# Row scales read back by three plain transfers; low halves of the attention weights made in one operation, with V loaded to both halves of the partitions

## The chip, the cores and the metric

The kernel runs on one core of a Trainium2 chip. The metric is the device time of one execution in microseconds, as the median of several runs. Five engines work side by side, each through its own list of instructions in order: PE (matrix multiplies, with PEld for its weight loads), DVE, ACT, POOL, and SP, which here issues every DMA.

## The reference

Attention with a threshold, followed by a feed-forward layer:

```python
# q, k, v: (8, 8, 576, 64), all f32
scores = scale * np.matmul(q, k.transpose(0, 1, 3, 2))
thresh = np.max(scores, axis=-1, keepdims=True) - tau
scores = np.where(scores >= thresh, scores, -1000000000.0)
scores = scores - np.max(scores, axis=-1, keepdims=True)
attn = np.exp(scores)
attn = attn / (np.sum(attn, axis=-1, keepdims=True) + 1e-09)
attn_out = np.matmul(attn, v)
...
x = attn_out.transpose(0, 2, 1, 3).reshape(8 * 576, 512)
h = x @ w_in                                   # w_in: (512, 2048)
g = np.maximum(h, 0.0) + np.log1p(np.exp(-np.abs(h)))
out = g @ w_out                                # w_out: (2048, 512)
```

## The kernel before

**Units and tiles.** A unit is one batch entry with two heads; there are 32 of them. A unit has 9 tiles of 128 query rows by 576 keys: tiles 0 to 3 belong to head 0, tiles 5 to 8 to head 1, and tile 4, called M, holds the last 64 rows of both heads. The main loop runs over 288 tiles. `PAT = "RemhlTfpSxfvwp"` gives the steps of one tile `t`, in the order in which they are written:

- `S`: the scores of tile t+3 on PE, into one of two PSUM buffers (`s`).
- `R`, `e`: the row maximum of tile t+2 (`negm`, DVE), its exponentials (`e_all`, ACT) and the threshold (`thr`, ACT).
- `m`: the mask of tile t+1 with its row sums (DVE, reads `s` and `e_all`); after it the PSUM buffer is free for new scores.
- `h`: `weights_hi` of tile t+1: POOL rounds the weights to f16.
- `l`: `weights_lo` of tile t: DVE makes the f16 remainder. Both go into one buffer `e16` of 1152 columns per row, shown in the profile as `e`.
- `T`: `weights_T` of tile t-1: a transposing DMA of that buffer into `eT`.
- `x`: `extras`: the work of the whole unit, spread over its tiles. `f`: a share of the feed-forward matmuls (`h`, `o`). `p`: one point; work that was put off by so many points is done there (two points in a tile).

The first six units (`s.whole`) go another way, with f32 weights transposed on PE, and do not use `weights_hi`, `weights_lo` and `weights_T`. In the other 26 units each block of 128 columns of `e16`, once transposed, is one matmul operand against 128 rows of `vt`: 64 keys as high halves and 64 other keys as low halves in the same block. So `weights_lo` writes the low halves of keys 0 to 511 to columns 640 to 1151 and those of keys 512 to 575 to columns 576 to 639, with two operations.

**V.** `load_v` loads V of the next unit into `vn` (one buffer for these units) in tile 0 of the running unit: one DMA to 128 partitions and two small ones for the last 64 keys. `top_v` takes its largest magnitude on DVE in tile 3, `split_v` scales it on ACT and splits it into f16 halves on POOL (`vt`) in tile 7. `load_v` of the unit after cannot be issued before POOL has read `vn`.

**Row scales.** After the last mask of a unit, `row_scales` makes the reciprocals; in the next unit they are transposed on PE (tile 1), copied by ACT to `rt`, written to HBM (`r_d`) and read back by `load_R` as `R`, each value to 64 partitions. `scale_x` on POOL multiplies the values by them 7 points later. `sums` puts the sum of tile t into column `ORDER[t]`, so that tile M stands last.

**Queries.** `queries` scales the next unit's queries of head 0 on ACT into the single buffer `q0` (shown as `q`), and `swap` exchanges its partition halves by two DMAs, `q<-q`. The scores of the next unit's first tile need them; `S` writes those three tiles ahead. The same for head 1 is `qT<-qT`.

**The order.** SP issues all DMAs in the order of the program, each one waiting for what it needs, so whatever stands behind a waiting DMA waits too. `Queue` and the priorities fix the order on DVE and ACT in the later part. Buffers of `e16`: `HB` in their own pool; from tile 84 on (`TE`) the even tiles of a unit use the three buffers `wi` of the weights instead.

Of the kernel before, what the change touches and what calls it, by code (L numbers as in the profile page):

```python
# [24 lines left out]
P = 128  # L25
# [38 lines left out]
def tile_kernel(ctx: ExitStack, tc: tile.TileContext, q, k, v, tau, w_in, w_out, out):  # L64
# [271 lines left out]

    def load_v(s):

        s.vn = apool.tile([P, 10, D], F32, tag="vt" if s.whole else "vn", bufs=2 if s.whole else 1, name=f"vn_{s.i}")
        load_rows(s, s.vn, v)  # L340
        for i in range(2):
            nc.sync.dma_start(
                s.vn.rearrange("p (h s) d -> p h s d", h=2)[i * SR:(i + 1) * SR, :, NC, :],
                v[s.b, 2 * s.hp:2 * s.hp + 2, SM:S, :].rearrange("h p d -> p h d"),
            )
# [188 lines left out]
    def weights_hi(s, t):  # L534

        pool, tag, bufs = (apool, "e16", HB) if now["tile"] < TE or t % 2 else (wpool, "wi", WB)
        s.e16[t] = h = pool.tile([P, 2 * S], F16, tag=tag, bufs=bufs, name=f"e16_{s.i}_{t}")
        nc.gpsimd.tensor_scalar(out=h[:, 0:S], in0=s.e[t], scalar1=2.0 ** 15, scalar2=1.0, op0=ALU.mult, op1=ALU.mult)  # L538

    def weights_lo(s, t):  # L540
        h, e = s.e16[t], s.e.pop(t)
        for i, o in ((slice(0, SM), slice(S + SR, 2 * S)), (slice(SM, S), slice(S, S + SR))):
            vec.scalar_tensor_tensor(out=h[:, o], in0=e[:, i], scalar=2.0 ** 15, in1=h[:, i],
                                     op0=ALU.mult, op1=ALU.subtract)

    def weights_T(s, t):
        if t in (0, M):
            j = int(t == M)
            s.eT[j] = apool.tile([P, 9, S], F16, tag="eT", bufs=2, name=f"eT_{s.i}_{j}")
        h = s.e16.pop(t)  # L550
        if t == M:
            for j in range(2):
                nc.sync.dma_start_transpose(s.eT[j][:, :, SM:S], h[j * SR:(j + 1) * SR])
            return
        j, c = divmod(t, NC + 1)
        nc.sync.dma_start_transpose(s.eT[j][:, :, c * P:(c + 1) * P], h)

    def values(s, g):
        if g == 0:
            s.xp = apool.tile([P, S], F32, tag="xp", bufs=NX, name=f"xp_{s.i}")  # L560
        j, x0 = g // 2, g % 2 * HS
        o = ps_g.tile([P, 512], F32, tag="g", name=f"pv_{s.i}_{g}")
        order = (0, 5, 1, 6, 2, 7, 3, 8, 4)
        for n, c in enumerate(order):
            nc.tensor.matmul(o[:, 0:HS], s.vt[:, 5 * j + (c if c <= NC else c - NC - 1), :],  # L565
                             s.eT[j][:, c, x0:x0 + HS], start=(n == 0), stop=(n == 8))
# [30 lines left out]
    def load_R(s):  # L597
        s.R = apool.tile([P, S], F32, tag="R", bufs=1, name=f"R_{s.i}")
        rows = s.r_d.rearrange("a p -> (a p)")
        for a, n in ((0, SM), (2 * SM, SR)):  # L600
            nc.sync.dma_start(s.R[:, a and SM:(a and SM) + n],
                              rows[a:a + 2 * n].rearrange("(j n) -> j n", j=2)[:, None, :].to_broadcast([2, D, n]))
# [330 lines left out]
    for s in units:  # L933
# [123 lines left out]
```

## Time and profile before

| | |
|---|---|
| median of 3 runs | 1413.39 us (1407.13 to 1413.59) |
| profiled execution, its own time | 1408.86 us |
| its span | 1407.1 us |
| PE busy | 1281.8 us, 91% |
| DVE busy | 1031.4 us, 73% |
| POOL busy | 920.9 us, 65% |
| ACT busy | 894.3 us, 64% |
| mean granted TensorE clock | 0.968 |

Tiles of the split units (from the seventh on) run from about 233 to 1257 us; ahead of that are the whole units and the preparation of the feed-forward weights, behind it feed-forward work alone. In a view by windows each engine has its busy time in the stretch, then come the granted TensorE clock, the mean busy share of the 16 DMA engines and what they moved. A row of a timeline has start, length, engine, line and operation, and in brackets how long the engine idled before it and what ended that. Instructions made through `Queue` all have its line, L154, and are told apart by their tiles.

### The profile page before, as it was taken

To read this page: it belongs to the slowest core of one execution; us is meant where nothing else is said; L and a number is where in the kernel's file an instruction comes from. 1 tells how busy PE (TensorE), PEld (TensorE's weight loads), DVE (VectorE), ACT (ScalarE), POOL (GpSimd) and SP (SyncE) were. 2 spreads that over 40 slices of the span, in tenths; PEclk is the share of its full clock that TensorE was granted. 3 is DMA by queue.
4 is the path that set the end of the run, shared out by engine and by line. 5 is a ranking of instruction groups with operands and counts; after the bars stand their busy time and mean duration, and the time that the engine had idled before them with its cause. 6 is when DMAs were issued, how large, how long until landed. Compare 5 with 4: busy or idle time off the path is not lost.

```text
span 1407.1 us, 21600 instructions
## 1 busy us (share of the span) xinstructions
PE 1281.8 (91%) x7094; PEld 759.2 (54%) x7094; DVE 1031.4 (73%) x1955; ACT 894.3 (64%) x1695; POOL 920.9 (65%) x1007
## 2 busy tenths in 40 slices
PE   6888898778989898999999999899999999999998
PEld 4555554344555555555555555555665765554455
DVE  6777766598987797789888898789787788761011
ACT  6666687556676667666776666566876667663222
POOL 2566878587776676667766676668767678546242
PEclk9988799999999999999999999999999999999999
DMA  4535333665876778777876786778766755651010
GB/s 140 143 107 126 116 82 95 118 101 109 164 123 115 119 138 140 122 126 127 148 131 116 120 159 125 119 122 160 117 118 114 142 100 124 97 77 40 0 38 16
DMA packets 354369, 158.15 MB, mean 112 GB/s; under 512 B 309297, under 2 KB 335313, under 8 KB 354257
## 3 DMA queue, kind: packets, MB, share of 16 engines
q1 hardware_dynamic: 354256, 156.77, 58.8%
q8 instruction: 56, 0.92, 0.3%
q14 instruction: 57, 0.46, 0.1%
HBM read 56.62 MB, written 10.63 MB: 48 GB/s over the span
## 4 chain that ended last, share of the span: by engine, by line
PE 34%; DVE 24%; ACT 15%; POOL 9%; issue 9%; DMA 6%; SPq 1%; DVEq 0%; POOLq 0%; ACTq 0%
PE o L751 12%; PE h L687 10%; DVE e L154 8%; PE s L455 6%; DVE e_all L154 6%; ACT L154 4%; DVE negm L154 4%; ACT st L154 4%; DMA q<-q 4%; PE pv L565 3%; ACT e_all L154 2%; DVE acc L154 2%; PE pv L524 2%; POOL g L178 2%; DVE xp L154 1%
## 5 line engine op out<-in xcount | busy, mean ns | idle before, releaser
L751 PE MATMUL o<-w_o,g 128*128 128x512 f16 x1728 | 419.3, 389 | 4.8 <-POOL g L178 2.3
L538 POOL TENSOR_SCALAR e<-e_all 128x576 f16<-128x576 f32 x234 | 226.2, 967 | 223.2 <-DVE e_all L154 220.9
L687 PE MATMUL h<-xh,w_i 128*128 128x512 f16 (+1 forms) x1280 | 363.0, 361 | 5.2 <-ACT xp L154 3.5
L154 DVE SCALAR_TENSOR_TENSOR e<-e_all,e 128x512 f16<-128x512 f32 x468 | 343.1, 772 | 14.3 <-POOL e L538 14.2
L154 ACT ACTIVATE e_all<-s,negm 128x576 f32<-128x576 f32 x288 | 213.4, 741 | 208.0 <-DVE negm L154 205.8
L687 PEld LDWEIGHTS <-w_i 128*128 128x128 f16 x1920 | 180.1, 98 | 166.6 <-issue 11.4
L154 DVE TENSOR_REDUCE negm<-s 128x1 f32<-128x576 f32 x288 | 214.6, 746 | 73.5 <-PE s L455 72.6
L154 DVE SCALAR_TENSOR_TENSOR e_all<-s,thr,e_all 128x576 f32<-128x576 f32 x288 | 232.6, 808 | 45.4 <-ACT thr L154 45.2
L751 PEld LDWEIGHTS <-g 128*128 128x128 f16 x1728 | 162.2, 100 | 186.1 <-issue 17.1
L687 PE MATMUL h<-xl,w_i 128*128 128x512 f16 (+1 forms) x640 | 230.9, 361 | 0.5 <-POOL xl L178 0.5
L455 PE MATMUL s<-kT,q 128*128 128x288 f32 x768 | 160.7, 336 | 68.5 <-DVE e_all L154 32.9
L154 DVE SCALAR_TENSOR_TENSOR acc<-o,c,acc 128x512 f32<-128x512 f32 x108 | 80.1, 743 | 164.2 <-PE o L751 146.3
L455 PEld LDWEIGHTS s<-kT,q 128*128 128x128 f32 x768 | 117.5, 198 | 116.5 <-DVE e_all L154 69.9
L178 POOL TENSOR_TENSOR g<-st,g 128x512 f16<-128x512 f32 x144 | 173.7, 1209 | 6.2
L154 ACT ACT_TABLE_LOAD x119 | 152.7, 1283 | 7.8 <-PE h L687 4.1
L177 POOL TENSOR_SCALAR g<-st 128x512 f16<-128x512 f32 x144 | 90.9, 634 | 96.6 <-ACT st L154 96.3
L565 PE MATMUL pv<-eT,vt 128*128 128x288 f16 x936 | 136.7, 291 | 3.8 <-DVE xp L154 3.5
L154 ACT ACTIVATE st<-h,c 128x512 f32<-128x512 f32 x144 | 91.1, 683 | 70.1 <-PE h L687 69.4
L455 PE MATMUL s<-kT,qT 128*128 128x288 f32 x512 | 107.5, 333 | 10.8 <-DVE e_all L154 10.0
L154 ACT COPY xp<-pv 64x288 f32<-64x288 f32 (+3 forms) x134 | 50.6, 382 | 95.0 <-PE pv L565 87.1
L565 PEld LDWEIGHTS <-vt 128*128 128x128 f16 x936 | 86.6, 99 | 38.1 <-issue 7.1
L154 ACT ACTIVATE st<-st,c 128x512 f32<-128x512 f32 x144 | 96.1, 715 | 2.1
(105 smaller groups left out, 1556.9 us busy)
## 6 DMA issues: line engine op xcount, KB each, us to landing
q<-q SPq DMA_DIRECT2D x62, 192.0 KB
kn<-in_k_dram SPq DMA_DIRECT2D x32, 256.0 KB
qn<-in_q_dram SPq DMA_DIRECT2D x32, 256.0 KB
vn<-in_v_dram SPq DMA_DIRECT2D x32, 256.0 KB
wc_i<-in_moe_w_in_dram SPq DMA_DIRECT2D x16, 512.0 KB
R<-r_d SPq DMA_DIRECT2D x32, 256.0 KB
wc_o<-in_moe_w_out_dram SPq DMA_DIRECT2D x16, 512.0 KB
qT<-qT SPq DMA_DIRECT2D x62, 128.0 KB
```

The costliest lines, as they stand in the source:

```text
L154: i = getattr(self.eng, name)(*args, **kwargs)
L177: nc.gpsimd.tensor_scalar(out=hi, in0=x, scalar1=1.0, scalar2=1.0, op0=ALU.mult, op1=ALU.mult)
L178: nc.gpsimd.tensor_tensor(out=lo, in0=x, in1=hi, op=ALU.subtract)
L455: nc.tensor.matmul(sp[:, hf, 0:HS], lhs, s.kT[j][:, hf * HS:(hf + 1) * HS], start=(m == 0), stop=(m == len(parts) - 1))
L524: nc.tensor.matmul(o[0:D, 0:n], s.vn[k_, 5 * j + c, :], h[k_, c, 0:n], start=(c == 0), stop=(c == NC))
L538: nc.gpsimd.tensor_scalar(out=h[:, 0:S], in0=s.e[t], scalar1=2.0 ** 15, scalar2=1.0, op0=ALU.mult, op1=ALU.mult)
L565: nc.tensor.matmul(o[:, 0:HS], s.vt[:, 5 * j + (c if c <= NC else c - NC - 1), :], s.eT[j][:, c, x0:x0 + HS], start=(n == 0), stop=(n == 8))
L687: nc.tensor.matmul(bank[:, i * u.T:(i + 1) * u.T], wi[g, cc][:, a, e], x[cc], start=(cc == 0 and m == 0), stop=(cc == NCC - 1 and m == 2))
L751: nc.tensor.matmul(o, u.g[fc][m // 2][:, sl], wo[fc][:, m % 2, :], start=(n == 0), stop=(n == 3 * QF - 1))
```

## The change

1. `load_R` reads the scales with three DMAs, each from a run of `r_d` to 64 partitions, where two DMAs read two runs at a time to 2 x 64 partitions. `ORDER` is gone: the sum of tile t stands in column t.
2. `e16` becomes 9 blocks of 64 high and 64 low halves of the same 64 keys, and `weights_lo` is one operation.
3. Each block so needs the same 64 rows of V in both halves of the partitions. `load_v` of the 26 units has four DMAs of 64 partitions and two small ones; `vn` grows from 10 to 18 slots of 64 columns, and so does `vt`. `top_v` reads all of it. `split_v` is done for one head in tile 6 and for the other in tile 8.
4. `values` takes the nine chunks in their order.
5. `HB` goes from 5 to 3.

```diff
-HB = 5
+HB = 3
...
+        s.vn = apool.tile([P, 2, 9, D], F32, tag="vn", bufs=1, name=f"vn_{s.i}")
         for i in range(2):
+            for j in range(2):
+                src = v[s.b, 2 * s.hp + j]
+                nc.sync.dma_start(
+                    s.vn[i * SR:(i + 1) * SR, j, 1:9, :].rearrange("p (n c) d -> p n (c d)", n=2),
+                    src[0:SM, :].rearrange("(n p c) d -> p n (c d)", n=2, c=NC))
+            nc.sync.dma_start(s.vn[i * SR:(i + 1) * SR, :, 0, :],
+                              v[s.b, 2 * s.hp:2 * s.hp + 2, SM:S, :].rearrange("h p d -> p h d"))
...
-    def split_v(s):
-        s.vt = apool.tile([P, 10, 2 * D], F16, tag="vt", bufs=2, name=f"vt_{s.i}")
-        act.activation(s.vn, s.vn, AF.Copy, scale=v_scale[:, s.i:s.i + 1])
-        halves(s.vt[:, :, 0:D], s.vt[:, :, D:2 * D], s.vn)
+    def split_v(s, j):
+        if s.whole:
+            return
+        if j == 0:
+            s.vt = apool.tile([P, 2, 9, 2 * D], F16, tag="vt", bufs=2, name=f"vt_{s.i}")
+        vj = s.vn[:, j]
+        act.activation(vj, vj, AF.Copy, scale=v_scale[:, s.i:s.i + 1])
+        halves(s.vt[:, j, :, 0:D], s.vt[:, j, :, D:2 * D], vj)
...
     def weights_lo(s, t):
-        h, e = s.e16[t], s.e.pop(t)
-        for i, o in ((slice(0, SM), slice(S + SR, 2 * S)), (slice(SM, S), slice(S, S + SR))):
-            vec.scalar_tensor_tensor(out=h[:, o], in0=e[:, i], scalar=2.0 ** 15, in1=h[:, i],
-                                     op0=ALU.mult, op1=ALU.subtract)
+        h = s.e16[t]
+        vec.scalar_tensor_tensor(out=h[:, :, 1, :], in0=s.e.pop(t).rearrange("p (c n) -> p c n", n=SR),
+                                 scalar=2.0 ** 15, in1=h[:, :, 0, :], op0=ALU.mult, op1=ALU.subtract)
...
     def load_R(s):
-        for a, n in ((0, SM), (2 * SM, SR)):
-            nc.sync.dma_start(s.R[:, a and SM:(a and SM) + n],
-                              rows[a:a + 2 * n].rearrange("(j n) -> j n", j=2)[:, None, :].to_broadcast([2, D, n]))
+        for j, a, n, x0 in ((0, 0, S, 0), (1, S, SR, SM), (1, S + SR, SM, 0)):
+            nc.sync.dma_start(s.R[j * D:(j + 1) * D, x0:x0 + n], rows[a:a + n].partition_broadcast(D))
...
-            times = ((s.i - 1, 0), (s.i - 1, 3), (s.i - 1, 7))
+            times = ((s.i - 1, 0), (s.i - 1, 3), (s.i - 1, 6), (s.i - 1, 8))
```

Two places where the lists of instructions differ. The first is SP around the read-back of the row scales in unit 18 (`r_d`, `R`; `e_18_3` and `e_18_4` are weights of tiles 3 and M, `q_95` is the buffer `q0`). Before:

```order
L594 DMA r_d_114<-rt_7789 9x128
L556 DMA_TRANSPOSE eT_0_7763<-e_18_2_7759 128x9x128
L601 DMA R_7809<-r_d_114 128x1x512
L601 DMA R_7809<-r_d_114 128x1x64
L556 DMA_TRANSPOSE eT_0_7763<-e_18_3_7798 128x9x128
L553 DMA_TRANSPOSE eT_0_7763<-e_18_4_7848 128x9x64
L553 DMA_TRANSPOSE eT_1_7960<-e_18_4_7848 128x9x64
L332 DMA qn_8120<-in_q_dram 128x2x256
L328 DMA qn_8120<-in_q_dram 128x1x64
L421 DMA q_95<-q_95 64x768
L422 DMA q_95<-q_95 64x768
```

And now, on SP at the same place:

```order
L614 DMA R_7796<-r_d_114 64x576
L614 DMA R_7796<-r_d_114 64x64
L614 DMA R_7796<-r_d_114 64x512
L570 DMA_TRANSPOSE eT_0_7751<-e_18_3_7786 128x9x128
L566 DMA_TRANSPOSE eT_0_7751<-e_18_4_7836 128x9x64
L567 DMA_TRANSPOSE eT_1_7945<-e_18_4_7836 128x9x64
L332 DMA qn_8105<-in_q_dram 128x2x256
L328 DMA qn_8105<-in_q_dram 128x1x64
L437 DMA q_95<-q_95 64x768
L438 DMA q_95<-q_95 64x768
```

The order behind the read-back is the same; two `R` transfers became three of other shapes, and `q<-q` still stands behind the transposes of tile M.

The second place is POOL at the boundary between units 17 and 18, where `vt` is made and `load_v` is released. Before:

```order
L538 TENSOR_SCALAR e_17_8_7632<-e_all 128x576
L177 TENSOR_SCALAR vt_7655<-vn_7315 128x10x64
L538 TENSOR_SCALAR e_18_0_7673<-e_all 128x576
L178 TENSOR_TENSOR vt_7655<-vn_7315,vt_7655 128x10x64
L127 TENSOR_SCALAR k_19_7741<-kn_7659 128x9x64
L134 TENSOR_TENSOR k_19_7741<-kn_7659,k_19_7741 128x9x64
L538 TENSOR_SCALAR e_18_1_7723<-e_all 128x576
```

And now, on POOL at that boundary:

```order
L177 TENSOR_SCALAR vt_7600<-vn_7303 128x9x64
L552 TENSOR_SCALAR e_17_8_7622<-e_all 128x9x64
L178 TENSOR_TENSOR vt_7600<-vn_7303,vt_7600 128x9x64
L552 TENSOR_SCALAR e_18_0_7658<-e_all 128x9x64
L177 TENSOR_SCALAR vt_7600<-vn_7303 128x9x64
L127 TENSOR_SCALAR k_19_7727<-kn_7644 128x9x64
L178 TENSOR_TENSOR vt_7600<-vn_7303,vt_7600 128x9x64
L134 TENSOR_TENSOR k_19_7727<-kn_7644,k_19_7727 128x9x64
L552 TENSOR_SCALAR e_18_1_7710<-e_all 128x9x64
```

Four `vt` operations of 576 columns stand there in place of two of 640, and the last reading of `vn` comes one operation of `k` and two of `vt` behind `e_18_0`, where it came right behind it.

More of the change, by code (lines that the diff above doesn't have):

```diff
@@ L337, in load_v @@
     def load_v(s):
-        s.vn = apool.tile([P, 10, D], F32, tag="vt" if s.whole else "vn", bufs=2 if s.whole else 1, name=f"vn_{s.i}")
-        load_rows(s, s.vn, v)
-        for i in range(2):
[L342 to L345, printed above, removed]
+        if s.whole:
+            s.vn = apool.tile([P, 10, D], F32, tag="vt", bufs=2, name=f"vn_{s.i}")
+            load_rows(s, s.vn, v)
+            for j in range(2):
+                nc.sync.dma_start(
+                    s.vn.rearrange("p (h s) d -> p h s d", h=2)[j * SR:(j + 1) * SR, :, NC, :],
+                    v[s.b, 2 * s.hp:2 * s.hp + 2, SM:S, :].rearrange("h p d -> p h d"),
+                )
+            return
+        s.vn = apool.tile([P, 2, 9, D], F32, tag="vn", bufs=1, name=f"vn_{s.i}")
+        for i in range(2):
+            for j in range(2):
+                src = v[s.b, 2 * s.hp + j]
+                nc.sync.dma_start(
+                    s.vn[i * SR:(i + 1) * SR, j, 1:9, :].rearrange("p (n c) d -> p n (c d)", n=2),
+                    src[0:SM, :].rearrange("(n p c) d -> p n (c d)", n=2, c=NC))
+            nc.sync.dma_start(s.vn[i * SR:(i + 1) * SR, :, 0, :],
+                              v[s.b, 2 * s.hp:2 * s.hp + 2, SM:S, :].rearrange("h p d -> p h d"))
     def top_v(s):
         tops = cpool.tile([P, 1], F32, tag="vtop", bufs=2, name=f"vtop_{s.i}")
-        vec.tensor_reduce(tops, s.vn.rearrange("p s d -> p (s d)"), axis=AX.X, op=ALU.max, apply_absolute_value=True)
+        vn = s.vn.rearrange("p s d -> p (s d)" if s.whole else "p h s d -> p (h s d)")
+        vec.tensor_reduce(tops, vn, axis=AX.X, op=ALU.max, apply_absolute_value=True)
         def spread():
@@ L362, in top_v @@
         defer(2, spread)
-    def split_v(s):
-        s.vt = apool.tile([P, 10, 2 * D], F16, tag="vt", bufs=2, name=f"vt_{s.i}")
-        act.activation(s.vn, s.vn, AF.Copy, scale=v_scale[:, s.i:s.i + 1])
-        halves(s.vt[:, :, 0:D], s.vt[:, :, D:2 * D], s.vn)
+    def split_v(s, j):
+        if s.whole:
+            return
+        if j == 0:
[3 more added lines that the diff above has]
+        halves(s.vt[:, j, :, 0:D], s.vt[:, j, :, D:2 * D], vj)
     def split_k(s):
@@ L474, in mask @@
             out=e2, in0=s.sp.pop(t)[:, :, 0:HS], scalar=s.m.pop(t)[1], in1=e2, op0=ALU.is_ge, op1=ALU.mult,
-            accum_out=s.sums[:, ORDER[t]:ORDER[t] + 1]))
+            accum_out=s.sums[:, t:t + 1]))
     GROUPS = ((0, ((0, 0, P), (1, 0, P))), (0, ((2, 0, P), (3, 0, P), (M, 0, SR))),
@@ L549, in weights_T @@
             s.eT[j] = apool.tile([P, 9, S], F16, tag="eT", bufs=2, name=f"eT_{s.i}_{j}")
-        h = s.e16.pop(t)
+        h = s.e16.pop(t).rearrange("p c i n -> p (c i n)")
         if t == M:
-            for j in range(2):
-                nc.sync.dma_start_transpose(s.eT[j][:, :, SM:S], h[j * SR:(j + 1) * SR])
+            nc.sync.dma_start_transpose(s.eT[0][:, :, SM:S], h[0:SR])
+            nc.sync.dma_start_transpose(s.eT[1][:, :, SM:S], h[SR:P])
             return
@@ L562, in values @@
         o = ps_g.tile([P, 512], F32, tag="g", name=f"pv_{s.i}_{g}")
[L563 to L566, printed above, removed]
+        for c in range(9):
+            slot = 0 if c == 8 else 1 + 4 * (c % 2) + c // 2
+            nc.tensor.matmul(o[:, 0:HS], s.vt[:, j, slot, :], s.eT[j][:, c, x0:x0 + HS], start=(c == 0), stop=(c == 8))
         defer(1, lambda: values_out(s, g, o))
@@ L940, in tile_kernel @@
         else:
-            times = ((s.i - 1, 0), (s.i - 1, 3), (s.i - 1, 7))
-        for at_, f in zip(times, (load_v, top_v, split_v)):
+            times = ((s.i - 1, 0), (s.i - 1, 3), (s.i - 1, 6), (s.i - 1, 8))
+        for at_, f in zip(times, (load_v, top_v, lambda x: split_v(x, 0), lambda x: split_v(x, 1))):
             plan.setdefault(at_, []).append(lambda f=f, s=s: f(s))
```

6 lines of the change are left out of this document (3 added, 3 removed).

## Prediction

> **What bounds the kernel now.** I read the page first, for the engines and the chain that ended last.
>
> ```profile
> PE 1281.8 (91%) x7094; PEld 759.2 (54%) x7094; DVE 1031.4 (73%) x1955; ACT 894.3 (64%) x1695; POOL 920.9 (65%) x1007
> PE 34%; DVE 24%; ACT 15%; POOL 9%; issue 9%; DMA 6%; SPq 1%; DVEq 0%; POOLq 0%; ACTq 0%
> PE o L751 12%; PE h L687 10%; DVE e L154 8%; PE s L455 6%; DVE e_all L154 6%; ACT L154 4%; DVE negm L154 4%; ACT st L154 4%; DMA q<-q 4%; PE pv L565 3%; ACT e_all L154 2%; DVE acc L154 2%; PE pv L524 2%; POOL g L178 2%; DVE xp L154 1%
> ```
>
> PE is the fullest engine, but it carries only a third of the chain. Two entries of the chain belong to what is changed: `DVE e`, the low halves, with 8%, and `DMA q<-q`, the swap of the queries, with 4%. A share of the chain is not a gain, so next come the stages (columns: PE, PEld, DVE, ACT and POOL busy, clock, DMA share, GB/s).
>
> ```profile
> 0.00:240.00 240.00, 198.46 (x1026) 125.42 (x1027) 169.15 (x346) 168.81 (x402) 152.31 (x171) 0.93 0.42 117
> 240.00:400.00 160.00, 133.26 (x698) 74.99 (x697) 130.73 (x240) 96.28 (x178) 121.34 (x131) 0.95 0.66 117
> 400.00:1000.00 600.00, 554.52 (x3107) 329.16 (x3105) 504.32 (x948) 405.16 (x736) 414.90 (x449) 0.97 0.74 130
> 1000.00:1250.00 250.00, 244.10 (x1460) 150.55 (x1459) 198.10 (x368) 177.60 (x307) 170.90 (x187) 1.00 0.67 116
> ```
>
> What the change touches lies in the last three rows. PE idles 26.7 us in the first of them, 45.5 in the second, 5.9 in the third. The clock adds a loss: 0.95 of 160 us and 0.97 of 600 us are 8 and 18 us of full speed. Together 104 us, the most that any repair could give. From 1000 us on PE is at 98% of the time and full clock; there is nearly nothing to win there. The waits of PE, in 400 to 1000 us and then in 240 to 400 us, say whom it waits for:
>
> ```profile
> PE s L455 <- DMA q<-q: 26.7, 12, 3.2
> PE s L455 <- DVE e_all L154: 10.5, 20, 0.9
> ...
> PE s L455 <- DVE e_all L154: 11.2, 11, 3.1
> PE h L687 <- ACT xp L154: 3.5, 1, 3.5
> ```
>
> So in the long middle stage the swap of the queries ends most of PE's idle time, once per unit; in the stage ahead of it the mask on DVE does. Why is the swap late? SP's timeline of unit 18:
>
> ```profile
> 725.23 1.11 SPq L601 DMA_DIRECT2D R<-r_d  x2
> 726.84 6.06 SPq L556 DMA_TRANSPOSE eT<-e  x1
> 733.01 2.55 SPq L553 DMA_TRANSPOSE eT<-e  x2
> 735.65 0.54 SPq L332 DMA_DIRECT2D qn<-in_q_dram  x1
> 736.24 0.55 SPq L328 DMA_DIRECT2D qn<-in_q_dram  x1
> 736.88 0.53 SPq L421 DMA_DIRECT2D q<-q  x1
> ```
>
> The transpose behind the two `R` transfers takes 6.06 us to issue; one of tile M takes 1.3 (2.55 for two). From there to the swap the queue runs without a gap, so the swap is late by what that transpose lost. Windows over that stretch and over the swap show the DMA engines (last two columns):
>
> ```profile
> 727.00:728.00 1.00, 1.00 (x7) 0.70 (x6) 0.97 (x2) 0.98 (x2) 0.00 (x0) 1.00 0.13 51
> 729.00:730.00 1.00, 1.00 (x11) 0.73 (x8) 1.00 (x4) 0.97 (x3) 0.01 (x1) 1.00 0.13 51
> 737.00:739.00 2.00, 2.00 (x12) 0.90 (x9) 2.00 (x5) 1.97 (x4) 1.07 (x3) 1.00 0.84 232
> ```
>
> While `R` is read only 0.13 of the 16 engines are busy, that is two, at 51 GB/s; the 256 KB of `R` (128 x 512 values of 4 bytes) need 5.1 us at that rate, and the transpose stands until they are through. With the swap in flight, itself to 64 partitions, 0.84 of them move 232 GB/s. PE then waits, and its clock is lower in the window behind the wait:
>
> ```profile
> 741.40 0.50 PE L455 MATMUL s<-kT,q 128*128 128x288 f32 x2 [1.96 <-DMA q<-q]
> 742.00:746.00 4.00, 4.00 (x15) 1.64 (x14) 3.29 (x6) 2.58 (x6) 3.78 (x6) 0.57 0.63 125
> ```
>
> A wait of 1.96 us is followed by 4 us at a clock of 0.57: 1.7 us more.
>
> **The change part by part. Read-back of the scales.** The new transfers go to 64 partitions each with one run as their source. No row shows a broadcast read of that shape. One bound is today's rate, so no gain; the other is that of the window with the swap: 288 KB at 232 GB/s, 1.3 us instead of 5. I take the second, since the swap is also a transfer to 64 partitions and the two pairs of the old one fit the two busy engines. The transpose then falls from 6.06 to 1.3 us, 4.7 us less in the queue. But the two transposes behind it need the low halves of tile M, which DVE finishes at 731.1:
>
> ```profile
> 729.83 1.28 DVE L154 SCALAR_TENSOR_TENSOR e<-e_all,e 128x512 f16<-128x512 f32 x2
> ```
>
> So they could start at 731.1 instead of 733.0, and the swap moves up by 1.9 us, not 4.7. The 12 waits average 2.2 us; 1.9 off each leaves some of the longer ones. I take 20 of the 26.7 us, and of the clock's 18 us 15, because most waits get too short to matter: 35 us. Its bounds are 0 and 45. For the third transfer SP pays 0.55 us a unit.
>
> The Trainium skill speaks against such transfers: SBUF — State Buffer, "Door 1: The DMA port swizzle", says that 64 partitions reach only half of the ports, about 218 GB/s at best, and advises one transfer over 128 partitions. By that rule the 576 KB of V now loaded for a unit would take 2.7 us of the DMA engines, 1.3 more than to 128 partitions: 35 us over 26 units if nothing hid them, and the sum would be 1390. The window with 232 GB/s holds other transfers beside the swap, so this trace does not settle it.
>
> **Low halves in one operation.** Groups kept apart by shape, and then one window in which POOL did not hold DVE up:
>
> ```profile
> L154 DVE SCALAR_TENSOR_TENSOR e<-e_all,e 128x512 f16<-128x512 f32 x234 | 189.5, 810 | 14.3 <-POOL e L538 14.2
> L154 DVE SCALAR_TENSOR_TENSOR e<-e_all,e 128x64 f16<-128x64 f32 x234 | 171.6, 733 | 0.0
> L154 DVE SCALAR_TENSOR_TENSOR e<-e_all,e 128x512 f16<-128x512 f32 x1 | 0.7, 686 | 0.0
> L154 DVE SCALAR_TENSOR_TENSOR e<-e_all,e 128x64 f16<-128x64 f32 x1 | 0.2, 217 | 0.0
> L154 DVE TENSOR_TENSOR k<-kn,k 128x576 fp32r<-128x576 f32 x1 | 0.8, 758 | 1.9 <-ACT k L154 1.9
> ```
>
> (The last row is from the start of the kernel.) The 64 columns cost 733 ns on average though they need 217: the operation starts while POOL works and ends when POOL's does. An operation of 576 columns, read and written in pieces of 64, exists: 758 ns. To it I add what the first of the two loses now, 810 - 686 = 124 ns: 882. Bounds are 758 and 1543, the present sum. Saved 810 + 733 - 882 = 661 ns on 234 tiles: 155 us of DVE time, some 6 us of a unit's 37. Most of it is slack, for PE is the fuller engine. What can turn into time is PE's idle time outside the swap: 45.5 - 26.7 = 18.8 us in the middle, 26.7 ahead, 5.9 behind. I take half: 9 + 13 + 3 = 25 us, and half of the clock's 8 us in the stage 240 to 400: 29 us. Its bounds are 5 and 50.
>
> The same page of the Trainium skill, "Who interferes with whom", has a rule for this: DVE with two SBUF inputs and a POOL operation that reads SBUF exclude each other for the whole instruction. By it the new operation holds POOL up longer by the time of 64 columns and can still lose up to a POOL operation itself, so if it met POOL as the second operation does (733 - 217 = 516 ns lost), it would take 1274 ns, 40% of the saving would be left, and the sum would be 1372. The rows agree with the rule; which of the two losses the new operation has they cannot show.
>
> **V in both halves.** Rows of what grows:
>
> ```profile
> L178 POOL TENSOR_TENSOR vt<-vn,vt 128x640 f16<-128x640 f32 x26 | 40.5, 1556 | 1.3
> L177 POOL TENSOR_SCALAR vt<-vn 128x640 f16<-128x640 f32 x26 | 20.1, 775 | 2.6 <-ACT vn L154 2.6
> L134 POOL TENSOR_TENSOR k<-kn,k 128x576 fp32r<-128x576 f32 x31 | 44.0, 1420 | 2.0
> L127 POOL TENSOR_SCALAR k<-kn 128x576 fp32r<-128x576 f32 x31 | 21.8, 703 | 29.8 <-PE tr L388 20.5 <-DMA kn<-in_k_dram 9.0
> L154 ACT ACTIVATE vn<-vn,v_scale 128x640 f32<-128x640 f32 x26 | 21.3, 820 | 0.0
> L154 DVE TENSOR_REDUCE vtop<-vn 128x1 f32<-128x640 f32 x32 | 26.1, 815 | 2.5 <-DMA vn<-in_v_dram 1.9
> L154 ACT ACTIVATE e_all<-s,negm 128x576 f32<-128x576 f32 x288 | 213.4, 741 | 208.0 <-DVE negm L154 205.8 <-POOL vt L177 1.2
> ```
>
> POOL: two pairs of 576 columns, priced as those of `k`, against one of 640: 2 x (1420 + 703) - (1556 + 775) = 1.9 us a unit, 50 us in all. ACT: 2 x 741 - 820 = 0.7 us a unit. DVE: `vtop` over 1152 columns, at most 815 x 1152 / 640 = 1467, 0.65 us a unit, 17 us off the 155. POOL has 600 - 414.9 = 185 us idle in the middle stage, 11.6 for each of its 16 units, and that covers it on average. Where it shows is the boundary of units: the last reading of `vn` comes later, and SP stands at `load_v` until then.
>
> ```profile
> 713.21 1.40 POOL L178 TENSOR_TENSOR vt<-vn,vt 128x640 f16<-128x640 f32 x1
> 714.77 0.53 SPq L332 DMA_DIRECT2D vn<-in_v_dram  x1
> 715.36 1.38 SPq L342 DMA_DIRECT2D vn<-in_v_dram  x2
> ...
> 722.32 0.72 SPq L594 DMA_DIRECT2D r_d<-rt  x1
> 723.82 1.31 SPq L556 DMA_TRANSPOSE eT<-e  x1
> ```
>
> Already now `load_v` goes out 0.16 us after POOL is done at 714.61. In the new order 0.70 + 0.70 + 1.42 us stand behind `e_18_0` where 1.40 did, so SP is held 1.4 us longer, then issues three more transfers at some 0.6: 1.8 us. With `R`'s 0.55 this gives 3.8 us back of the 4.7, earlier in the unit. Behind it wait transposes of tiles 0 to 2, whose products come in tile 7. 0.9 us of the 4.7 are left, and SP has gaps on the way, 0.8 us behind `r_d` (723.04 to 723.82) and 0.5 behind `R` (726.34 to 726.84); together 2.2 us, just enough for the 1.9 of the swap. V itself has three tiles until `top_v`. Because of `HB` three buffers hold the weights in tiles 54 to 83, so a transpose held up there stops POOL. For all this together I charge 9 us; bounds 0 and 50 (all of POOL's work on the path).
>
> The order of chunks in `values` and of `sums` costs nothing: the same number of matmuls of the same shape. The tail after 1257 us keeps its work; its spare buffers from `e16` come round once in ten pairs.
>
> **Sum.** 1408.9 - 35 - 29 + 9 = 1354, say 1355 us, against the profiled execution's own 1408.86, which is 4.5 us below the median of 1413.39 and inside its runs.
>
> **Rivals.** (a) *The stall only moves.* The broadcast read is still done by few engines, or `load_v` takes the place of `R`: the 3.8 us given back are not caught up and the swap is as late as today. For it speaks how tight the queue is (2.2 us for 1.9), against it the two engines' share. Then only the low halves count: 1408.9 - 29 + 9 = 1389.
> (b) *The low halves are hidden anyway*: PE stays behind `thr` and `negm`, and only the swap's part comes: 1408.9 - 35 + 9 = 1383. For it: the mask ends only 10.5 us of PE's idle time in the middle.
> (c) *POOL at the boundary of units becomes the bound.* The four `vt` operations push the high halves of the unit's first tiles back, and low halves, transposes and masks wait behind. With all 50 us on the path and the swap no earlier: 1408.9 - 29 + 50 = 1430, slower. It decides from the point where the delay at a boundary exceeds the 11.6 us of slack that POOL has in a unit; 1.9 are added, which speaks against it.
> (d) Nothing measurable: what is won goes into waits for ACT.
>
> **How the numbers follow.** Forecast 0.58, (a) 0.17, (b) 0.08, (c) 0.11, (d) 0.06. Within 0.5%, some 7 us, is about what a measurement of this kernel cannot tell from no change. Faster are the forecast, (a) and (b): 0.83; the same (d): 0.06; slower (c): 0.11. The forecast's own range goes from 1330, where PE's idle time and clock after 240 us become those of the last stage (104 us less 2.4% of 1010, about 80), to 1378. The range to state reaches over (b) and (a) to 1395.
>
> **What would show it.** In the profile after: no transpose of some 6 us on SP, and a window with the DMA share well over 0.13 right after `R`; waits of PE for `q<-q` under 10 us in all; a clock of 0.99 in the middle; 234 operations of `e` at 0.8 to 0.95 us; POOL busy some 50 us more, less what it no longer loses. I am wrong if the long transposes are still there, if SP's waits at `load_v` exceed 3 us a unit, or if POOL's high halves wait for buffers in tiles 54 to 83.

## Result, and the profile after

The changed kernel takes 1374.17 us (median of 4 runs, 1372.50 to 1377.79) against 1410.26 us for the kernel before (4 runs, 1403.52 to 1413.59): ratio 0.9753, interval 0.9707 to 0.9800. Forecast were 1355 us in a range of 1330 to 1395. The profiled execution took 1377.79 us, its span is 1376.0 us, its mean granted clock 0.978.

From the page: busy time of each engine, then the shares of the chain that ended last.

```profile
PE 1268.2 (92%) x7094; PEld 758.5 (55%) x7094; DVE 938.0 (68%) x1721; ACT 908.5 (66%) x1721; POOL 981.5 (71%) x1059
PE 39%; POOL 21%; DVE 15%; issue 9%; ACT 9%; DMA 5%; SPq 1%; POOLq 0%; DVEq 0%; ACTq 0%
```

DVE lost 93 us of work, POOL gained 61, and POOL's share of the chain went from 9% to 21%, while DVE's went from 24% to 15%. Two later stages by windows (columns as before; the end of the second moves with the units, which now come earlier):

```profile
240.00:400.00 160.00, 129.00 (x668) 74.13 (x668) 121.71 (x208) 98.96 (x180) 121.07 (x130) 0.93 0.58 124
400.00:966.00 566.00, 535.42 (x3084) 323.22 (x3083) 447.24 (x798) 407.94 (x745) 448.07 (x479) 0.99 0.71 143
```

The stage from 1000 to 1250 us of before, the end of the split units, now starts at 966 us instead of 1000. In the middle stage PE idles 31 us instead of 45, and the clock is 0.99 instead of 0.97. The stage from 240 to 400 us gained nothing: PE idles 31 us there, 27 before. Not all of the 34 us were won in the middle, for the first mask of the split units already starts at 221 us instead of 231; the first experiment comes back to this. The waits of PE in the middle stage (total, times, longest):

```profile
PE tr L404 <- DVE xp L154: 19.3, 11, 4.0
...
PE s L471 <- DMA q<-q: 2.5, 4, 1.1
```

The wait for the swap of the queries, 26.7 us before, is 2.5 us. A new one of 19.3 us took its place: the transposes of `k` wait for DVE's `xp`. SP's timeline at the read-back in unit 18:

```profile
709.88 1.80 SPq L614 DMA_DIRECT2D R<-r_d  x3
711.78 1.30 SPq L570 DMA_TRANSPOSE eT<-e  x1
...
717.12 0.51 SPq L437 DMA_DIRECT2D q<-q  x1
```

The transpose behind `R` takes 1.30 us, where it took 6.06, and the swap follows the start of the read-back by 7.2 us instead of 11.7. By the trace's list of DMA packets the two large transfers of `R` move their data from 711.19 to 713.62 us, 2.4 us in all; before, it was from 726.55 to 732.63, 6.1 us. Windows over this:

```profile
711.00:712.00 1.00, 1.00 (x10) 0.71 (x8) 1.00 (x3) 0.97 (x2) 0.22 (x1) 1.00 0.51 165
712.00:713.00 1.00, 1.00 (x9) 0.61 (x8) 0.36 (x1) 0.98 (x3) 1.00 (x2) 1.00 0.35 105
```

With what else is in flight the DMA engines are 0.51 and 0.35 busy, at 165 and 105 GB/s, where 0.13 of them moved 51 GB/s. Groups of instructions by shape (count, busy time, mean ns of one, idle time before them):

```profile
L154 DVE SCALAR_TENSOR_TENSOR e<-e_all,e 128x576 f16<-128x576 f32 x234 | 233.1, 996 | 39.5 <-POOL e L552 39.2
L178 POOL TENSOR_TENSOR vt<-vn,vt 128x576 f16<-128x576 f32 x52 | 68.9, 1325 | 2.2
L177 POOL TENSOR_SCALAR vt<-vn 128x576 f16<-128x576 f32 x52 | 40.1, 771 | 3.5 <-ACT vn L154 3.3
```

One operation for the low halves costs 996 ns on average instead of 810 + 733. DVE idles 39.2 us in front of it for POOL's high halves; it was 14.2. The split of V takes POOL 109.0 us instead of 60.6.

**The new wait.** POOL's timeline at the boundary of units 16 and 17 (units counted from 0, four to a batch entry), then DVE's and PE's:

```profile
648.31 0.67 POOL L177 TENSOR_SCALAR vt<-vn 128x576 f16<-128x576 f32 x1
649.06 1.80 POOL L178 TENSOR_TENSOR vt<-vn,vt 128x576 f16<-128x576 f32 x1
650.83 0.62 POOL L177 TENSOR_SCALAR xh<-xp 128x512 f16<-128x512 f32 x1
651.41 0.46 POOL L127 TENSOR_SCALAR q<-qn 128x320 fp32r<-128x320 f32 x1
651.84 1.17 POOL L178 TENSOR_TENSOR xl<-xp,xh 128x512 f16<-128x512 f32 x1
652.96 0.86 POOL L134 TENSOR_TENSOR q<-qn,q 128x320 fp32r<-128x320 f32 x1
653.79 1.30 POOL L552 TENSOR_SCALAR e<-e_all 128x576 f16<-128x576 f32 x2
655.06 1.17 POOL L177 TENSOR_SCALAR vt<-vn 128x576 f16<-128x576 f32 x1
656.31 1.27 POOL L178 TENSOR_TENSOR vt<-vn,vt 128x576 f16<-128x576 f32 x1
```

```profile
654.49 1.21 DVE L154 SCALAR_TENSOR_TENSOR e<-e_all,e 128x576 f16<-128x576 f32 x1 [3.06 <-POOL e L552]
655.62 0.63 DVE L154 TENSOR_SCALAR c<-p_i,sx 128x4 f32<-128x4 f32 x1
656.29 1.32 DVE L154 TENSOR_SCALAR c<-c 128x4 f32<-128x4 f32 x2
657.53 0.44 DVE L154 TENSOR_TENSOR xp<-pv,xp 64x288 f32<-64x288 f32 x1
```

```profile
658.02 0.37 PE L404 MATMUL tr<-identr,k 128*128 128x128 f32 x1 [4.03 <-DVE xp L154]
```

Two `vt` operations and four for `q` and for the feed-forward operand keep POOL from 648.31 to 653.79, and only then come the high halves. DVE stands 3.06 us at the low half that needs them. Then the second pair of `vt` follows on POOL, and beside it three small operations of DVE on the feed-forward tile `c` take 0.63 us and 1.32 us for two. Only behind them stands `xp`, for which PE's transposes of `k` wait 4.03 us. In the middle stage the wait comes some 7 us after the first mask of units 13, 17, 21 and 25, the second of each batch entry: 4.03 us three times, 3.59 once. PE's clock pays once more, as in these windows:

```profile
658.00:660.00 2.00, 1.98 (x6) 0.88 (x7) 1.97 (x5) 0.21 (x1) 1.43 (x2) 0.50 0.63 181
660.00:662.00 2.00, 2.00 (x6) 0.68 (x5) 1.80 (x5) 0.92 (x2) 1.75 (x2) 0.50 0.81 241
662.00:664.00 2.00, 2.00 (x10) 1.28 (x9) 0.29 (x1) 0.00 (x0) 0.00 (x0) 0.74 0.70 185
```

From 658 to 664 us PE is busy with a clock of 0.50, 0.50 and 0.74: 2 x (0.50 + 0.50 + 0.26) = 2.5 us lost behind a wait of 4.

### The profile page after: what moved, and what is told of

It is laid out like the page before. It is cut to its first block, busy times and chain, and to the rows that moved or that the text cites. A ratio compares the mean times of both kernels' runs of the same rounds, so it can differ in the third digit from the quotient of the medians.

```text
span 1376.0 us, 21746 instructions
## 1 busy us (share of the span) xinstructions
PE 1268.2 (92%) x7094; PEld 758.5 (55%) x7094; DVE 938.0 (68%) x1721; ACT 908.5 (66%) x1721; POOL 981.5 (71%) x1059
## 4 chain that ended last, share of the span: by engine, by line
PE 39%; POOL 21%; DVE 15%; issue 9%; ACT 9%; DMA 5%; SPq 1%; POOLq 0%; DVEq 0%; ACTq 0%
PE h L699 14%; PE o L763 11%; PE s L471 6%; DVE e L154 4%; DVE e_all L154 4%; POOL g L178 4%; POOL e L552 3%; PE pv L579 3%; DVE negm L154 3%; ACT L154 2%; POOL g L177 2%; ACT st L154 2%; DMA eT<-e 2%; PE pv L538 2%; POOL q L134 1%
## 5 line engine op out<-in xcount | busy, mean ns | idle before, releaser
L763 PE MATMUL o<-w_o,g 128*128 128x512 f16 x1728 | 410.1, 382 | 6.3 <-POOL g L178 2.9
L699 PE MATMUL h<-xh,w_i 128*128 128x512 f16 (+1 forms) x1280 | 369.2, 365 | 8.7 <-ACT xp L154 4.8
L552 POOL TENSOR_SCALAR e<-e_all 128x576 f16<-128x576 f32 x234 | 219.6, 940 | 173.2 <-DVE e_all L154 161.0
L154 DVE SCALAR_TENSOR_TENSOR e<-e_all,e 128x576 f16<-128x576 f32 x234 | 233.1, 996 | 39.5 <-POOL e L552 39.2
L178 POOL TENSOR_TENSOR g<-st,g 128x512 f16<-128x512 f32 x144 | 176.8, 1230 | 6.3
```

The lines of the kernel that those rows point to most:

```text
L154: i = getattr(self.eng, name)(*args, **kwargs)
L178: nc.gpsimd.tensor_tensor(out=lo, in0=x, in1=hi, op=ALU.subtract)
L552: nc.gpsimd.tensor_scalar(out=h[:, :, 0, :], in0=s.e[t].rearrange("p (c n) -> p c n", n=SR), scalar1=2.0 ** 15, scalar2=1.0, op0=ALU.mult, ...
L699: nc.tensor.matmul(bank[:, i * u.T:(i + 1) * u.T], wi[g, cc][:, a, e], x[cc], start=(cc == 0 and m == 0), stop=(cc == NCC - 1 and m == 2))
L763: nc.tensor.matmul(o, u.g[fc][m // 2][:, sl], wo[fc][:, m % 2, :], start=(n == 0), stop=(n == 3 * QF - 1))
```

## Experiments

Medians are of 4 runs where no other number stands, ratios are to the kernel before on the same chip, with intervals. The changed kernel itself was timed on another occasion, so differences to its 1374.17 us carry its own interval of about 6 us either way. The kernel before had a median of 1410 us on that occasion and of 1413 to 1417 us on the others; where a difference of ratios gives another number than a difference of medians, it stands in brackets.

### The read-back alone

```diff
 # the kernel before
-ORDER = ...
+ORDER = (0, 1, 2, 3, 4, 5, 6, 7, 8)
     def load_R(s):
-        for a, n in ((0, SM), (2 * SM, SR)): ...
+        for j, a, n, x0 in ((0, 0, S, 0), (1, S, SR, SM), (1, S + SR, SM, 0)):
+            nc.sync.dma_start(s.R[j * D:(j + 1) * D, x0:x0 + n], rows[a:a + n].partition_broadcast(D))
```

> The kernel before with one change: the row scales are read back by three transfers to 64 partitions each, and the sums stand in the order of the tiles. Low halves, V and HB are those of before. Theory A (the stall of SP behind the two-engine read-back is the larger term, priced 35 us): no transpose over 4 us on SP, PE's waits for q<-q in the middle stage fall from 26.7 to under 8 us, and the time is 30 to 38 us below before, 1372 to 1380. Rival (the stall goes, but DVE then sets the pace, because its low halves still cost 1543 ns a tile): the waits for q<-q fall too, PE's waits for the mask rise, and the time is only 10 to 20 us below before.

Measured: 1369.19 us (1366.84 to 1370.46), ratio 0.9682 [0.9652, 0.9713]. Its middle stage and PE's waits in it:

```profile
400.00:960.00 560.00, 528.26 (x3036) 314.85 (x3037) 503.52 (x932) 394.16 (x719) 403.92 (x435) 1.00 0.67 136
```

```profile
PE s L455 <- DVE e_all L154: 19.0, 30, 0.9
...
PE s L455 <- DMA q<-q: 1.3, 2, 1.0
```

The swap's wait is 1.3 us and the clock 1.00. The wait for the mask is 19.0 us, where it was 10.5, so PE's idle time in the stage falls by 14 us, not by the 25 that the swap gave back. With all else of the change left out the kernel is no slower than with all of it: the three plain transfers are worth 3.2%, some 45 us, by themselves.

A part of that lies ahead of the split units. The stretch up to their first mask, before and with the read-back alone, then two waits of before in it:

```profile
0.00:231.00 231.00, 190.24 (x983) 120.57 (x983) 162.77 (x329) 161.69 (x386) 146.37 (x164) 0.93 0.43 119
0.00:219.00 219.00, 185.34 (x984) 118.20 (x984) 162.13 (x329) 162.41 (x387) 148.11 (x164) 0.96 0.44 126
```

```profile
POOL xp L606 <- DMA R<-r_d: 11.3, 3, 4.7
SPq L612 <- POOL xp L606: 25.5, 4, 8.5
```

The whole units read their row scales back too. POOL stood 11.3 us at its product with `R`, and SP 25.5 us behind that product, with the swap later in its list; in the read-back alone the two are 0.9 and 6.6 us. The same work takes 12 us less there. All kernels with the new read-back reach the first mask of the split units at 216 to 221 us, the three with the old one at 231 to 232.

### All but the read-back

```diff
 # the changed kernel
-        for j, a, n, x0 in ((0, 0, S, 0), (1, S, SR, SM), (1, S + SR, SM, 0)): ...
+        for a, n in ((0, SM), (2 * SM, SR)): ...          # load_R of before, with ORDER
```

> The kernel after, but with the row scales read back by the two transfers of before (and the sums in the order that these need). Low halves in one operation, V in both halves and HB = 3 stay. Theory A: long transposes of some 6 us and PE's waits for q<-q (over 20 us) are back, and the time is 0 to 12 us below before, 1398 to 1410, since POOL's work at the unit boundaries takes most of what the merged operation gives. Rival (the merged operation is the larger term): 20 us or more below before.

Measured: 1444.64 us (1442.32 to 1446.54), ratio 1.0217 [1.0186, 1.0249]: slower by 31 us, which was not expected. SP's timeline in one unit, then PE's wait for the swap in the middle stage:

```profile
594.69 1.10 SPq L616 DMA_DIRECT2D R<-r_d  x2
595.90 6.54 SPq L572 DMA_TRANSPOSE eT<-e  x1
...
606.43 0.52 SPq L437 DMA_DIRECT2D q<-q  x1
```

```profile
PE s L471 <- DMA q<-q: 48.5, 14, 6.0
```

The long transpose is back: 25 transposes take over 4 us, in the changed kernel none. The swap is later than in the kernel before: 48.5 us of waits, 3.5 on average, where it was 26.7. Averaged over units 10 to 25 and counted from the first mask of the unit, `load_v` with its six transfers goes out at 5.1 us instead of 2.6, the read-back at 16.9 instead of 15.1 and the swap at 27.8 instead of 26.3. Rival (a) has the mechanism of this kernel, at too kind a price (1389 us): the swap is not as late as in the kernel before but 1.5 us later. As long as the broadcast read stalls the queue, what is added to SP ahead of it arrives at PE. So with the rest of the change in place the new read-back is worth 1444.6 - 1374.2 = 70 us (66), where alone it was worth 45.

### The low halves in two operations again

```diff
 # the changed kernel
-        vec.scalar_tensor_tensor(out=h[:, :, 1, :], in0=e, ..., in1=h[:, :, 0, :], ...)
+        for c in (slice(0, 8), slice(8, 9)):
+            vec.scalar_tensor_tensor(out=h[:, c, 1, :], in0=e[:, c], ..., in1=h[:, c, 0, :], ...)
```

> The kernel after, but the low halves are made in two operations again, of 512 and of 64 columns, in the new layout; all else as after. It tells what the merged operation is worth by itself. By the prediction's step (661 ns of DVE time a tile, about half of PE's idle time) 20 to 29 us above after, 1394 to 1403. Rival (DVE is not what bounds after, POOL and the unit boundaries are): under 8 us above after.

Measured: 1401.36 us (7 runs, 1399 to 1405), ratio 0.9921 [0.9894, 0.9947]. The two shapes:

```profile
L154 DVE SCALAR_TENSOR_TENSOR e<-e_all,e 128x512 f16<-128x512 f32 x234 | 216.9, 927 | 26.7 <-POOL e L552 26.6
L154 DVE SCALAR_TENSOR_TENSOR e<-e_all,e 128x64 f16<-128x64 f32 x234 | 169.9, 726 | 0.0
```

Against the changed kernel this is 1401.4 - 1374.2 = 27 us (24): the value of the merged operation, 927 + 726 - 996 = 657 ns on 234 tiles. Against the read-back alone it is 1401.4 - 1369.2 = 32 us (34): the price of V in both halves with all that comes with it, since this kernel has the new read-back, the new V, the new blocks of `e16`, three buffers and two operations as before. The blocks by themselves do not make the operation dearer: the shortest of 512 columns takes 675 ns here and 672 in the read-back alone; the means are 927 and 832.

### Where the 32 us are

**Half of V's split left out.** Only the first head's V is scaled and split, and the values of both heads are multiplied with it (that line is not shown).

```diff
     def split_v(s, j):
+        if j == 1:
+            return
```

> The kernel after, but only the first head's V is scaled and split, and both heads multiply by it: ACT and POOL do one group of 576 columns a unit, where before had one of 640 and after has two of 576. Left out: V of the second head. Transfers as after. Theory C (what the change gives back is POOL's doubled split at the unit boundaries): the units at the batch boundaries (13, 17, 21, 25) take 36 to 38 us instead of 41, and the time is 12 to 20 us below after, 1354 to 1362. Rival D (it is SP's longer list of V transfers): within 5 us of after.

Measured: 1348.81 us, ratio 0.9556 [0.9516, 0.9595]: 25 us (28) less than the changed kernel. POOL's busy time falls from 981.5 to 930.0 us, and the wait of PE at the boundary shown above is 2.65 us instead of 4.03. DVE and PE there:

```profile
637.85 1.21 DVE L154 SCALAR_TENSOR_TENSOR e<-e_all,e 128x576 f16<-128x576 f32 x1 [3.05 <-POOL e L554]
638.98 0.22 DVE L154 TENSOR_SCALAR c<-p_i,sx 128x4 f32<-128x4 f32 x1
639.23 0.38 DVE L154 TENSOR_SCALAR c<-c 128x4 f32<-128x4 f32 x2
639.51 0.44 DVE L154 TENSOR_TENSOR xp<-pv,xp 64x288 f32<-64x288 f32 x1
640.01 0.28 PE L406 MATMUL tr<-identr,k 128*128 128x128 f32 x1 [2.65 <-DVE xp L154]
```

DVE waits 3.05 us for the high half, as in the changed kernel: ahead of it POOL has the first pair of `vt` and the same four operations. The difference comes behind that. With no second pair beside them the operations on `c` are short, and `xp` starts 1.66 us after the low half instead of 3.04; these 1.38 us are the whole difference of the two waits. The clock adds to it: in the changed kernel it fell to 0.50 for 3.4 us or more behind three of the four waits of the middle stage, here behind none. The 2.65 us that are left go with the first pair and the four operations ahead of the high half; in the read-back alone, where `vt` stands elsewhere, the wait is 0.8 to 1.2 us. This edit also lets `load_v` go out 4 us earlier in a unit (2.1 us after the first mask instead of 6.2), so it does not tell POOL from SP by itself.

**V by fewer transfers.** The first 512 keys come by two transfers to 128 partitions instead of four to 64; that each row of V stands in both halves of the partitions is left out.

```diff
-            for j in range(2): ...            # four of 64 partitions
+        for n in range(2):
+            nc.sync.dma_start(s.vn[:, :, 1 + NC*n:1 + NC*(n+1), :]..., v[..., 0:SM, :]...)   # two of 128
```

> The kernel after, but the first 512 keys of V come by two transfers to 128 partitions, each with both heads, instead of four to 64: the same bytes and pieces of 1 KB, two DMAs fewer a unit. Left out: the right place of V's rows. Rival D (SP's list, or transfers to 64 partitions, cost what after gives back): 8 us or more below after. Theory C: within 4 us of after, since SP has room once the read-back is fast.

Measured: 1369.83 us, ratio 0.9695 [0.9647, 0.9742]: 4 us (8) less, and the interval overlaps that of the changed kernel. SP's longer list and the shape of V's transfers are worth that or nothing. PE's waits of 4.0 us for `xp` are all there.

**Three buffers for the weights.** `HB` set to 3 alone, once in the kernel before and once with the read-back alone.

```diff
-HB = 5
+HB = 3
```

> The kernel before with HB = 3 instead of 5 and nothing else. If the three buffers stop POOL in tiles 54 to 83, unit 8 (tiles 72 to 80), which is 5.1 us longer in the kernel after, is 4 to 5 us longer here too, and the time is 4 to 8 us above before. Rival: the buffers are free in time, the time is that of before within 2 us, and the 5.1 us of unit 8 come from the work at its boundary.

> The kernel before with the new read-back and HB = 3. Of the 32 us that V in both halves and HB = 3 together cost, POOL's split has 25 and two V transfers of six 4. If the rest is HB, this is 3 to 6 us above the kernel with the new read-back alone (1369), with units 8 and 9 longer than their 34.7 and 37.1 us. Rival (three buffers are enough): within 2 us of it, units 8 and 9 as they were.

Measured: 1415.11 us (10 runs, 1408 to 1425), ratio 1.0014 [0.9987, 1.0041], and 1367.26 us, ratio 0.9679 [0.9661, 0.9698]. Neither differs from the kernel that it is made from. Fewer buffers cost nothing that can be measured.

So of the 32 us (34) the second split, with what hangs on it, is 25 (28) and the shape of V's transfers 4 (8) or nothing. The first is rather an upper bound, for this run leaves out 54 us of POOL's work where the change had added 48. Whether anything remains these differences cannot tell.

**Less work for POOL, nothing left out.** ACT rounds V's high halves, and POOL makes only the low ones; in the changed kernel and in the one with the read-back alone.

```diff
-        halves(hi, lo, vj)
+        act.copy(hi, vj)
+        nc.gpsimd.tensor_tensor(out=lo, in0=vj, in1=hi, op=ALU.subtract)
```

> The kernel after, but the high halves of V are rounded by ACT (a copy to f16) and POOL makes only the low halves; nothing is left out. POOL loses 2 x 0.77 = 1.5 us a unit of the 2.1 us that the run with one head's split left out, ACT gains about as much, at 66% of its time. Theory C (POOL's split of V is what the change gives back, 25 us for 2.1 us a unit): some 18 us below after less a few for ACT, 1355 to 1364, and so below the kernel with the new read-back alone (1369). Rival (ACT, with its table loads, is as tight as POOL at the boundaries): 1368 or more.

> The kernel before with the new read-back and, as in the run beside it, V's high halves rounded by ACT; low halves of the weights in two operations, V as before. If POOL matters only where the change has doubled its split, this is within 5 us of 1369. If any microsecond off POOL at the unit boundaries is worth as much (0.78 us a unit here, against 2.1 us for 25), it is about 9 us below, 1358 to 1363, and the lead of the merged operation is smaller than it looks.

Measured: 1359.91 us, ratio 0.9607 [0.9567, 0.9648], and 1361.15 us, ratio 0.9620 [0.9584, 0.9656]. These two ran on another chip than the rest, so differences by ratios count here. By their pages POOL is busy 947.3 us in the first and 903.5 in the second, DVE 931.3 and 1027.6.

POOL gives up two operations of 771 ns a unit in the first and one of 776 in the second. The first gains 14 us (20) on the changed kernel, the second 8 (9) on the read-back alone. Both are faster than the kernel before and the changed one, and they do not differ from each other: DVE's 96 us less bring nothing that can be measured, as long as POOL has V twice.

### Moving the work in time

```diff
 # load of V, its maximum, the two splits; (unit, tile)
-            times = ((s.i - 1, 0), (s.i - 1, 3), (s.i - 1, 6), (s.i - 1, 8))
+            times = ((s.i - 1, 4), (s.i - 1, 7), (s.i, 1), (s.i, 2))      # later
+            times = ((s.i - 1, 7), (s.i, 0), (s.i, 2), (s.i, 2))          # latest, meant to be behind the swap
```

Later:

> The kernel after with V loaded, its maximum taken and its split made later: load in tile 4, maximum in tile 7 of the unit ahead, the split of the two heads in tiles 1 and 2 of the unit itself, where POOL had gaps. Theory B (in every fourth unit POOL reaches the high halves of tiles 8 and 0 some 3 us late because the vt operations stand ahead of them; DVE's low halves, the additions to xp behind them and PE's transposes of k wait in turn, 4.0 us each time): the waits of 4.0 us at the starts of units 13, 17, 21 and 25 shrink below 1.5 us, those units take 36 to 38 us instead of 41, and the time is 10 to 18 us below after, 1356 to 1364. Rival (POOL has simply too much to do around these boundaries, so the wait only moves): within 4 us of after.

Measured: 1375.90 us, ratio 0.9724 [0.9687, 0.9761]: no gain, a miss. PE's waits in the middle stage:

```profile
PE s L471 <- DMA q<-q: 16.9, 12, 4.0
```

The waits of 4 us for `xp` are gone, as expected: the longest in this stage is 0.5 us. The swap's wait is back with 16.9 us; most of V's six transfers now stand between the read-back and the swap on SP.

Latest:

> The kernel after with V loaded in tile 7 of the unit ahead, behind the swap of the queries, its maximum in tile 0 and both splits in tile 2 of the unit itself. In the run with loads in tile 4 the waits of 4 us at the batch boundaries were gone, but the V transfers stood ahead of q<-q on SP and PE waited 19 us for it. Theory B with SP's order: both waits are small now (q<-q under 6 us, no wait of 4 us for xp), and the time is 12 to 20 us below after, 1354 to 1362, and below the kernel that changes the read-back alone (1369). Rival: POOL's extra 60 us show somewhere else, and the time is within 5 us of after.

Measured: 1403.51 us (10 runs, 1397 to 1410), ratio 0.9938 [0.9912, 0.9964]: a miss again. PE's wait for the swap in the middle stage, then SP in one unit:

```profile
PE s L471 <- DMA q<-q: 28.9, 15, 3.5
```

```profile
723.42 1.89 SPq L614 DMA_DIRECT2D R<-r_d  x3
...
727.13 1.33 SPq L352 DMA_DIRECT2D vn<-in_v_dram  x2
...
734.46 0.53 SPq L437 DMA_DIRECT2D q<-q  x1
```

V did not come behind the swap: in every unit of the trace three to six of its six transfers stand ahead of the swap on SP, as in the kernel with the later load. In the middle stage they wait 25.3 us for POOL's `q`, and the swap is issued 27.4 us after the first mask of its unit, where it was 25.6. So neither tile was free of the cost, and a load of V that does stand behind the swap is not tested.

## Why the prediction came out as it did

The sum was -35 - 29 + 9. Measured one by one the terms are about -45, -27 and +32, together -40; the two kernels' medians differ by 36, and the other 4 us are the medians of the kernel before on two occasions. The three are steps of one path, so their sum is no test of them: with the old read-back the other two parts cost 31 us together, behind the new one 5 (10).

**Read-back of the scales: the mechanism as forecast, one stage left out.** The stall vanished, and the swap moved up by what the low halves of tile M allow. In the read-back alone the last part of those low halves ends at 738.03 us and the swap starts 4.0 us later; before, 731.1 and 736.88, 5.8 us:

```profile
733.49 1.82 SPq L601 DMA_DIRECT2D R<-r_d  x3
...
738.09 2.52 SPq L553 DMA_TRANSPOSE eT<-e  x2
...
741.99 0.52 SPq L421 DMA_DIRECT2D q<-q  x1
```

1.8 us against 1.9 forecast; counted from the first mask and over units 10 to 25 it is 1.2. The 1.3 us taken for the transfer at 232 GB/s were too few, for it took 2.4; the window with that rate held loads of queries beside the swap. It cost nothing, since the transpose behind it took 1.30 us all the same.

What failed is "What the change touches lies in the last three rows". The whole units, in the first row, read their scales back in the same way, and the same work takes 12 us less there. From the first mask of the split units to that of the last unit the read-back alone takes 959 us instead of 989, 30 us less, against 35 forecast. (In all the two profiled executions differ by 38 us, the medians by 45.) Inside the 35 the shares were others: PE's idle time in the middle fell by 14 us, not by 20, because waits for the mask took the place of some for the swap, and the clock gave back all of its 18, not 15.

**Low halves in one operation: right, 27 (24) against 29.** The saving per tile was forecast as 661 ns and is 657 against the same kernel with two operations. The operation itself is dearer than the 882 ns forecast, 996, but so are its two parts in that kernel, 927 + 726 = 1653 against 1543 in the kernel before. The tile's own view (min, median, max) shows why a mean misleads:

```profile
L154 DVE SCALAR_TENSOR_TENSOR e<-e_all,e x234: 740/763/1942, 223.9 to 1221.1; 128x576 f16<-128x576 f32 x117
```

Half of the 234 take 763 ns or less, the bound from `k`'s row of 758; others take up to 1942 ns. The Trainium skill's rule in SBUF — State Buffer, "Who interferes with whom", is that a DVE operation with two SBUF inputs and a POOL operation that reads SBUF exclude each other; the trace agrees in having such a tail. The 1274 ns for an operation that always meets POOL were too much: 996 - 763 = 233 ns over the median were lost on average, not 516. Its sum of 1372 lies close to the result, but not for its reason, since this term measured what was forecast.

**V in both halves: the term that was far too small, 32 against 9.** The prices were right: the split takes POOL 109.0 - 60.6 = 48 us more, forecast 50, and ACT is busy 14 us more, forecast 18. "POOL has 185 us idle in the middle stage, and that covers it on average" was wrong as an argument on time. POOL's idle time lies elsewhere in the unit. The four `vt` operations come at the change of units, where `q` and the first high halves are queued too, and once per batch entry the feed-forward operand, and from 639.4 to 657.6 us POOL had none. That was rival (c), priced at 50 us and given 0.11 because 1.9 us are less than a slack of 11.6. It came true by half, 25 us for the second split, while the other two terms stood, and in part by another way: (c) has the high halves pushed back, which at the boundary shown is the work of the first pair; the second pair slows the operations of DVE beside it. By units it shows most at the second of each batch entry (units 13, 17, 21, 25), taken from the first mask of a unit to that of the next:

| | unit 13 | 17 | 21 | 25 |
|---|---|---|---|---|
| before | 40.9 us | 38.0 | 40.2 | 38.2 |
| read-back alone | 36.9 | 36.8 | 36.8 | 38.3 |
| changed kernel | 40.6 | 41.4 | 40.6 | 41.5 |
| half of V's split left out | 37.9 | 37.9 | 37.9 | 40.1 |

The other units from 10 to 24 take 33.0 to 35.5 us in the changed kernel and 35.3 to 35.7 in the read-back alone: the merged operation gains between boundaries, POOL gives it back at them. Of the time that leaving out half of V's split saves, 10 us lie in these four units and 9 us in units 7 to 9, at the start of the split units; the rest is spread, and some of it lies where no V is split.

**Luck.** The 10 us that the read-back brought beyond its price and the 23 us by which V was priced too low pull against each other. Without the first the forecast would have been off by about 30 us instead of 19.

**SP at `load_v`: held, with little to spare.** SP's waits there in the whole span:

```profile
SPq L352 <- POOL vt L178: 26.3, 15, 5.0
SPq L352 <- POOL k L127: 18.1, 10, 3.0
```

That is 44.4 us on 26 units, 1.7 each, under the 3 given as a limit. "2.2 us, just enough for the 1.9 of the swap" was enough, as 2.5 us of waits for the swap show. With the old read-back it was not, and with V's load later it was not either.

**V to 64 partitions.** What the Trainium skill has against it (SBUF — State Buffer, "Door 1: The DMA port swizzle": 64 partitions reach half of the ports) was weighed at 35 us if nothing hid them; the two transfers to 128 partitions gained 4 (8), with overlapping intervals. The slower transfers are hidden here, though whether each is slower no run shows by itself.

**Three buffers.** The last condition for a miss, high halves that wait for buffers, did not come: `HB` is worth nothing either way.

## What to carry to other kernels

An engine's idle time over a stage does not cover added work; look at its timeline in the stretch where the work will stand, and at who is queued behind it there. Price a part of a change by taking it alone and by taking it out alone: here one part brought the whole gain, 45 us alone and 70 when it was the part taken out, and the other two, of 27 and 32 us, cancelled each other. Look for a step that is changed in every stage in which it runs: 12 us came from a stage that the sum did not have. When a wait that ends PE's idle time once per unit goes, other waits take some of its place, while the clock that fell behind it comes back whole.

## What the runs showed of the hardware

- A read that gives two runs of HBM to 2 x 64 partitions kept 0.13 of the DMA engines busy at 51 GB/s for 6.1 us, and the transposing DMA issued behind it took 6.06 us to issue instead of 1.3. As three reads of one run to 64 partitions each, the data takes 2.4 us, issuing 1.80 us and the transpose behind them 1.30. The Trainium skill, DMA: Bandwidth & Descriptors, "Rules for kernel authors", says that an outermost dimension of a size c under 16 confines a DMA to at most c engines; with c of 2 that is 2/16 = 0.13, and the trace agrees. What it does to the transpose behind it only the trace told.
- A wait of 1.96 us was enough for the clock: 1.7 us more were lost behind it, and 2.5 behind the one of 4.03. The Trainium skill, TensorE: Matmul & The Clock Gate, "What's actually happening", has the clock halved after at least one idle window of some 3.4 us; here less did it. Nor does the length decide alone: with half of V's split left out the waits of 2.65 us were followed by a clock of 1.00. In these traces a drop inside the span lasts 3.41 us, 6.83 or 10.24, at 0.50.
- Beside a pair of POOL's `vt` operations three DVE operations of 4 columns took 0.63 us and 1.32 for two, without it 0.22 and 0.38.
- On POOL a microsecond taken off the split of V is worth less than one: 25 us for 26 x (1325 + 771) ns = 54 us of work together with 20 us of ACT's, 14 (20) for 40, 8 (9) for 20. A third to a half of what is taken off comes back as time, though POOL is busy only 71% of the span.
